# Scan chunks of 64 tokens in a fused Mamba-2 scan and maxout feed-forward kernel

One Trainium2 chip (trn2), one core. The metric is device time in microseconds (us) of that core, lower is better. The kernel before takes 296.08 us (median of 3 runs, 291.53 to 296.67).

## The reference

A state-space scan over 768 tokens (4 batches, 8 heads, head size 32, state size 16), then a feed-forward layer with the maximum of three products. Cut to what matters:

```python
# scan, per chunk of tokens (any chunk length gives the same y)
L = np.exp(cum[:, :, :, None] - cum[:, :, None, :]) * causal
M = np.einsum('bhin,bhjn->bhij', Cc, Bc) * L               # scores and decay
y_intra = np.einsum('bhij,bhjd->bhid', M, xc)              # "own tokens"
y_inter = np.einsum('bhin,bhnd->bhid', Cc, state) * np.exp(cum)[..., None]   # "old state"
state = decay_full * state + sum_j(B_j x_j * decay_from_j) # "new state"
# feed-forward
h = np.maximum(np.maximum(x @ w1, x @ w2), x @ w3)
return h @ w_out
```

## The kernel before

The tokens go through in six blocks of 128 tokens (all four batches, 512 columns), called 0 to 5. For block c+1 the scan is done in between the feed-forward work of block c. The steps of the scan are: transposes of B and C (`trB`, `trC`), scores, decay (loaded as broadcast rows, masked on GpSimd, exponentials on ScalarE), the product of scores and decay on VectorE, old state and own tokens into the y banks (I call the two together the **y visit**), and the new state. Each engine gets its work as one list, in the order of the program, and a piece that has to wait holds up what stands behind it (experiments 3 to 5 show three such cases, in which TensorE waited 0.84 us a block, 3.0 and 1.2 us in the changed kernel). A *bank* is a piece of the memory that TensorE writes its results to, a *tile* of TensorE the part of its array that a `tile_position` names, a *unit* a piece of feed-forward work of some 4.4 us. `Bd` is B times the decay to the end of the chunk (GpSimd), `E` the exponential of the summed decay (ScalarE), `Cd` is C times `E` (VectorE).

The parts that change and that matter here:

```python
    def decay_masks(c, bs):                       # GpSimd
        for b in bs:
            nc.gpsimd.affine_select(out=Ls[c][:, b], in_=Ls[c][:, b], ...)   # 128 x 1024 each

    def decay_part(c, b, g):                      # ScalarE, 4 heads of one batch
        for h in range(g * HALF, (g + 1) * HALF):
            nc.scalar.activation(L[:, b, h], L[:, b, h], AF.Exp, bias=..., scale=1.0)

    def scan_state(c, kind):                      # L456: 16 matmuls, four column tiles
        for b in range(NB):
            for r in range(NP):
                nc.tensor.matmul(out=A[r * PN:(r + 1) * PN, b], lhsT=st["Bd"][:, h:h + 2],
                    rhs=st["x"][:, h:h + 2], tile_position=(0, r * PN), ...)

    def scan_scores(c, b0, banks=None):           # L488: two batches a visit, four row tiles
        for i in range(2):
            for r, s in banks.items():
                nc.tensor.matmul(out=s[:, i], lhsT=st["BT"][rows, b],
                    rhs=st["CT"][rows, b], tile_position=(r * PN, 0), ...)

    def scan_old(c):                              # L511: 16 matmuls of 128 columns
        ...
                nc.tensor.matmul(out=ys[r // 2][q:q + 2 * D, b], lhsT=Sp[rows, b],
                    rhs=st["Cd"][rows, b], start=(b == 0), stop=False,
                    tile_position=(r * PN, q), ...)

    def scan_own(c, bs):                          # L524: 32 matmuls of 128 columns
        for b in bs:
            for h in range(NH):
                t, q = divmod(h, QH)
                nc.tensor.matmul(out=st["y"][t][q * D:(q + 1) * D, b],
                    lhsT=st["x"][:, b * NH + h], rhs=M[:, b, h],
                    tile_position=(0, q * D), ...)
```

(Shapes rearranged and arguments cut where marked by `...`.)

Of the kernel before, what the change touches and what calls it, by code (L numbers as in the profile page):

```python
# [19 lines left out]
def kernel(  # L20
# [19 lines left out]

    nc = tc.nc
# [3 lines left out]
    P = 128  # L45
# [14 lines left out]
    HB = BLK // 2  # L60
    MASKED = -32768.0
# [189 lines left out]


# [9 lines left out]
    def running(rows, lg, out):  # L262
        for w in range(out.shape[1]):
            nc.vector.tensor_tensor_scan(
                out=out[:, w], data0=keep[0:rows], data1=lg[:, w], initial=0.0,
                op0=ALU.mult, op1=ALU.add)

    def from_last(rows, cum, name):

        fj = const.tile(list(cum.shape), FP32, name=name)  # L270
        for w in range(cum.shape[1]):
            nc.scalar.activation(
                fj[0:rows, w], cum[0:rows, w], AF.Exp, bias=cum[0:rows, w, P - 1:P], scale=-1.0)
        return fj
# [20 lines left out]

    Ls = {}

    def decays(c):
        Ls[c] = att.tile([P, NB, NH, P], FP32, tag="L", name="L")
        return Ls[c]  # L300
# [60 lines left out]
    L0, spread = decays(0), {}  # L361
# [6 lines left out]
    running(P, lg0, cum0)  # L368
# [5 lines left out]
    def decay_load(c, pairs=(0, 2)):  # L374
        L = decays(c) if 0 in pairs else Ls[c]
        for b in pairs:
            nc.sync.dma_start(
                out=L[:, b:b + 2].rearrange("j b h i -> j (b h) i"),
                in_=cums[b * NH:(b + 2) * NH, c, :].partition_broadcast(P))
# [7 lines left out]
    def decay_masks(c, bs):  # L387
        for b in bs:
            nc.gpsimd.affine_select(  # L389
                out=Ls[c][:, b], in_=Ls[c][:, b], pattern=[[0, NH], [1, P]],  # L390
                compare_op=ALU.is_ge, fill=MASKED, base=0, channel_multiplier=-1)

    def decay_part(c, b, g):
        L = Ls[c]
        for h in range(g * HALF, (g + 1) * HALF):
            nc.scalar.activation(  # L396
                L[:, b, h], L[:, b, h], AF.Exp,
                bias=ncum[c][:, b * NH + h:b * NH + h + 1], scale=1.0)
# [51 lines left out]
    def scan_state(c, kind):  # L450
        st = blocks[c]
        A = kind([HN, NB, 2, D], "A")
        for b in range(NB):
            for r in range(NP):
                h = b * NH + 2 * r
                nc.tensor.matmul(  # L456
                    out=A[r * PN:(r + 1) * PN, b].rearrange("p g d -> p (g d)"),
                    lhsT=st["Bd"][:, h:h + 2].rearrange("j h n -> j (h n)"),
                    rhs=st["x"][:, h:h + 2].rearrange("j h d -> j (h d)"),
                    start=(b == 0), stop=True, tile_position=(0, r * PN),  # L460
                    skip_group_check=True)
        return lambda: scan_sum(c, A)

    def scan_sum(c, A):
        st = blocks[c]
        states[c + 1] = Sn = att.tile([HN, NB, 2, D], FP32, tag="S", bufs=3, name="S")
        nc.vector.tensor_tensor(  # L467
            out=Sn, in0=A,
            in1=parity.unsqueeze(1).unsqueeze(3).to_broadcast([HN, NB, 2, D]), op=ALU.mult)
        if c > 0:  # L470
            old = att.tile([HN, NB, 2 * D], FP32, tag="old", name="old")
            nc.gpsimd.tensor_tensor(
                out=old, in0=states[c].rearrange("p b g d -> p b (g d)"),
                in1=st["E"][:, :, P - 1:P].to_broadcast([HN, NB, 2 * D]), op=ALU.mult)
            nc.gpsimd.tensor_tensor(  # L475
                out=Sn.rearrange("p b g d -> p b (g d)"),
                in0=Sn.rearrange("p b g d -> p b (g d)"), in1=old, op=ALU.add)

    def scan_scores(c, b0, banks=None):

        st = blocks[c]
        if banks is None:
            banks = {r: att_bank([P, 2, 2, P], "s") for r in range(NP)}
        for i in range(2):
            b = b0 + i
            for r, s in banks.items():
                rows = slice(r * PN, (r + 1) * PN)
                nc.tensor.matmul(  # L488
                    out=s[:, i].rearrange("j g i -> j (g i)"), lhsT=st["BT"][rows, b],
                    rhs=st["CT"][rows, b].rearrange("p g i -> p (g i)"),  # L490
                    start=(i == 0), stop=True, tile_position=(r * PN, 0), skip_group_check=True)
        return banks

    def scan_weight(c, b0, r, s):
        M = Ls[c][:, b0:b0 + 2, 2 * r:2 * r + 2]
        nc.vector.tensor_tensor(out=M, in0=s, in1=M, op=ALU.mult)  # L496

    def scan_weights(c, b0, banks):
        for r, s in banks.items():
            scan_weight(c, b0, r, s)  # L500

    def scan_old(c):

        st = blocks[c]
        st["y"] = ys = [att_bank([P, NB, P], "y") for _ in range(KD)]
        Sp = states[c]
        for b in range(NB):
            for r in range(NP):
                rows = slice(r * PN, (r + 1) * PN)
                q = r % 2 * 2 * D  # L510
                nc.tensor.matmul(  # L511
                    out=ys[r // 2][q:q + 2 * D, b],
                    lhsT=Sp[rows, b].rearrange("p g d -> p (g d)"), rhs=st["Cd"][rows, b],
                    start=(b == 0), stop=False, tile_position=(r * PN, q),
                    skip_group_check=True)

    def scan_own(c, bs):
# [3 lines left out]
        for b in bs:  # L521
            for h in range(NH):
                t, q = divmod(h, QH)
                nc.tensor.matmul(  # L524
                    out=st["y"][t][q * D:(q + 1) * D, b], lhsT=st["x"][:, b * NH + h],
                    rhs=M[:, b, h], start=False, stop=True,
                    tile_position=(0, q * D), skip_group_check=True)
# [17 lines left out]
    def scan_y(c):  # L545
        yT[c] = ffn.tile([P, KD, BLK], FP32, tag="yT", name="yT")
        for t in range(KD):
            nc.scalar.copy(out=yT[c][:, t], in_=blocks[c]["y"][t].rearrange("p b i -> p (b i)"))

    def scan_sums(c):  # L550
# [3 lines left out]
        late = [blocks[c]["y"][k].rearrange("p b i -> p (b i)")[:, r * HB:(r + 1) * HB]  # L554
                for k in range(2) for r in range(2)]
# [4 lines left out]
            for k, (a1, a0) in enumerate((  # L560
                (late[1], y11), (late[3], t[:, 0]), (late[3], y12), (late[2], t[:, 1]))))
# [141 lines left out]
    def hidden_sums(c, eng, fs):  # L703
# [4 lines left out]
        if c not in token_sums:  # L708
            if c < NC - 2:
                t = ffn.tile([P, 3 * NQ, 2, P], FP32, tag="hs", bufs=1, name="hs")  # L710
            else:
                t = att.tile([P, NB, NH, P], FP32, tag="L", name="L").rearrange(
                    "p b (h u) i -> p (b h) u i", u=2)
# [83 lines left out]
    def add_downs(c):  # L797
        if c == 0:
            downs.extend((u, i, f) for u in range(2) for f in range(0, NF, 2) for i in range(2))
        elif c < NC - 2:  # L800
            downs.extend((c, u, which) for u, which in (
                (0, (1,)), (0, (6,)), (0, (5, 7)), (0, (2, 3, 4)), (1, (1, 6)), (1, (5, 7)),
                (1, (2, 3, 4))))
# [85 lines left out]
    running(R, lg, a_sb)  # L889
# [17 lines left out]
    s01 = scan_scores(0, 0)  # L907
    s23 = scan_scores(0, 2, {r: ffn_bank([P, 2, 2, P], "s") for r in (2, 3)})
    state_sum = scan_state(0, att_bank)
    ncums_tp = turned(R, a_sb, "ncums", ffn_bank)  # L910
    scan_weights(0, 0, s01)
# [9 lines left out]
    s23 = scan_scores(0, 2, {r: att_bank([P, 2, 2, P], "s") for r in (0, 1)})  # L921
    sign()
    scan_weights(0, 2, s23)
# [7 lines left out]
    def decay_list(c):  # L931
        return [(c, b + b0, g) for b0 in (0, 2) for g in range(2) for b in range(2)]
# [27 lines left out]
    def transposed(n, both=True):  # L960
# [3 lines left out]
        if n < NC - 1:  # L964
            scan_bd(n)

    def scores(n, b):
        for r, s in scan_scores(n, b).items():
            later.append(lambda r=r, s=s: scan_weight(n, b, r, s))

    for n in range(NF * 3):
# [17 lines left out]
        if n in (13, 14, 16, 17):  # L989
            pop(2)  # L990
# [10 lines left out]
        if n == 1:  # L1001
            fj = from_last(R, a_sb, "fj")
# [10 lines left out]
        if n == 9:  # L1013
            decay_masks(1, (2, 3))
        if n in (5, 7, 9, 11, 13, 14, 15, 16):
# [4 lines left out]
        if n == 12:  # L1020
            scan_e(1)
            scan_cd(1)
            scores(1, 0)
        if n == 15:
            shared["att"] = False
            scores(1, 2)
# [7 lines left out]
    scan_own(1, range(NB))  # L1034
    scan_y(1)
    scan_sums(1)
    later.append(scan_state(1, att_bank))
# [8 lines left out]
    X1 = ["tc", "D", "DD", "s0", "DD", "s2", "A", "y", "DD"]  # L1046
    Y1 = ["", "", "D", "", "", "D", "", "D", ""]
    P1 = [(1, 0, 0), (1, 0, 0), (1, 0, 1), (1, 1, 2), (1, 0, 0), (1, 1, 2), (1, 1, 1), (1, 0, 2),
          (1, 0, 2)]
    D1 = [(0, 0), (0, 0), (2, 0), (2, 0), (2, 0), (2, 0), (0, 2), (0, 1), (0, 2)]  # L1050
    K1 = {0: (0, (0, 1)), 2: (0, (2, 3)), 4: (1, (0, 1)), 6: (1, (2, 3))}
    X2 = ["t", "s0", "D", "s2", "D", "y", "D", "D", "D"]
    Y2 = ["D", "D", "", "", "", "", "", "", ""]
    P2 = [(1, 0, 1), (1, 1, 3), (0, 0, 1), (1, 1, 2), (1, 0, 0), (1, 0, 0), (9, 0, 0), (1, 0, 0),
          (1, 0, 0)]
    D2 = [(0, 0), (1, 0), (1, 0), (1, 0)] + 5 * [(0, 1)]
    K2 = {3: (1, (0, 1)), 5: (1, (2, 3))}
    X3, Y3, P3 = 9 * [""], 9 * [""], 9 * [(1, 0, 0)]

    for c in range(1, NC):  # L1060
# [4 lines left out]
        for k in range(NW):  # L1065
# [20 lines left out]
            elif x == "A":  # L1086
                later.append(scan_state(n, att_bank))
# [5 lines left out]
            elif x == "s0":  # L1093
                scores(n, 0)
            elif x == "s2":
                scores(n, 2)
            elif x == "y":
                scan_old(n)
                scan_own(n, range(NB))
                scan_y(n)  # L1100
                scan_sums(n)
                if 1 < c < NC - 2:
                    later.append(scan_state(n, att_bank))
# [13 lines left out]
            if not (1 < c < NC - 1 and k == 2):  # L1117
                flush()
# [41 lines left out]
```

## Time and profile before

| | before |
|---|---|
| time, median of 3 | 296.08 us (fast 291.53, slow 296.08 and 296.67) |
| span of the profiled (slow) execution | 294.2 us |
| TensorE busy | 283.0 us, 96% |
| TensorE program | 17 packets of instructions on queue 8 |

The program has two kinds of execution. In the slow kind TensorE runs at half clock (granted clock 0.50 in the profile) for 10.24 us near 16 us, which costs about 5 us. The kernel before took 290.5 to 291.8 us without that half clock and 296.1 to 297.1 us with it, so I compare executions with full clock at the start only with each other, and take 291.2 for the kernel before.

### The profile page before, as it was taken

The numbers are of one execution on the slowest core, as the hardware profiler recorded it, in microseconds if no ns is written. First come the engines' busy times: TensorE is split into PE (matmuls) and PEld (weight loads), VectorE is DVE, ScalarE is ACT, GpSimd is POOL, SyncE is SP. The second block draws the span as 40 slices with busy tenths as digits, with TensorE's granted clock in tenths as the row PEclk, the third lists the DMA queues.
The fourth block names the chain that finished last, engine by engine and source line by source line (L and its number), as shares of the span: only waits on it lengthen the run. The fifth ranks groups of instructions, "written<-read, shape, count | busy, mean of one in ns | idle before, by whom it ended". The sixth has DMA issues, their size and how long they took to land.

```text
span 294.2 us, 5768 instructions
## 1 busy us (share of the span) xinstructions
PE 283.0 (96%) x2204; PEld 226.0 (77%) x2204; DVE 214.0 (73%) x427; ACT 119.6 (41%) x323; POOL 113.4 (39%) x132
## 2 busy tenths in 40 slices
PE   6679999999999999999999999999999999999995
PEld 4557435478887788878987878988878988989885
DVE  2752867988698578896867796776897766676682
ACT  3933687834665546333426243335331201011101
POOL 5241638367997535920004940003630203030300
PEclk9957999999999999999999999999999999999999
DMA  7979989989884009971006693001001001000103
GB/s 88 218 255 301 217 144 176 246 171 219 232 140 67 2 21 253 142 88 38 2 0 180 177 128 57 2 0 36 2 0 38 2 1 36 2 1 0 38 0 107
DMA packets 105035, 28.15 MB, mean 96 GB/s; under 512 B 75312, under 2 KB 101936, under 8 KB 105008
## 3 DMA queue, kind: packets, MB, share of 16 engines
q1 hardware_dynamic: 104560, 27.53, 46.5%
q8 instruction: 17, 0.28, 0.4%
q10 hardware_dynamic: 448, 0.26, 0.3%
q14 instruction: 10, 0.08, 0.1%
HBM read 24.54 MB, written 3.24 MB: 94 GB/s over the span
## 4 chain that ended last, share of the span: by engine, by line
PE 84%; DVE 7%; DMA 3%; SPq 2%; issue 1%; ACT 1%; POOL 0%; DVEq 0%; ACTq 0%; POOLq 0%
PE sumB L633 25%; PE sumA L633 18%; PE o L743 16%; PE up L583 8%; PE s L488 4%; PE o L819 4%; PE y L524 3%; DMA raw_x<-in_x_dram 3%; PE y L511 2%; PE up L575 2%; PE y L535 1%; SPq L130 1%; PE A L456 1%; DVE rb L675 1%; DVE m L678 1%
## 5 line engine op out<-in xcount | busy, mean ns | idle before, releaser
L633 PE MATMUL sumA<-yT,w 128*128 128x256 f32 x180 | 55.4, 389 | 0.0
L396 ACT ACTIVATE L<-L,ncums 128x128 f32<-128x128 f32 x160 | 50.2, 393 | 2.5 <-POOL L L389 2.5
L658 ACT COPY eu<-sumA 128x256 f32<-128x256 f32 x45 | 16.8, 373 | 75.3 <-PE sumA L633 68.7
L633 PE MATMUL sumB<-rb 128*128 128x256 f32 x180 | 46.3, 379 | 0.0
L633 PEld LDWEIGHTS sumB<-rb 128*128 128x128 f32 x180 | 34.1, 190 | 4.8 <-DVE rb L558 0.2
L633 PEld LDWEIGHTS sumA<-yT,w 128*128 128x128 f32 x180 | 30.0, 190 | 6.7 <-issue 2.1
L496 DVE TENSOR_TENSOR L<-s,L 128x512 f32<-128x512 f32 x46 | 29.7, 680 | 2.8 <-PE s L488 2.5
L583 PE MATMUL up<-yT,w 128*128 128x512 f32 x64 | 29.1, 600 | 0.2 <-DVE w L193 0.2
L675 DVE TENSOR_TENSOR rb<-sumB,eu 128x512 f32<-128x512 f32 x30 | 20.7, 690 | 11.8 <-PE sumB L633 11.8
L659 DVE TENSOR_TENSOR eu<-sumA,eu 128x256 f32<-128x256 f32 x45 | 18.9, 420 | 14.2 <-ACT eu L658 14.0
L633 PE MATMUL sumB<-yT,rb 128*128 128x256 f32 x90 | 27.9, 391 | 0.3 <-DVE m L661 0.3
L190 POOL TENSOR_TENSOR w_u<-w_u,w_r 128x512 uint32<-128x512 uint32 x12 | 15.3, 1274 | 32.9 <-DVE w_u L184 14.9
L633 PE MATMUL sumA<-rb 128*128 128x256 f32 x90 | 26.8, 379 | 0.0
L633 PE MATMUL sumB<-rb,w 128*128 128x256 f32 x90 | 26.8, 379 | 0.0
L389 POOL TENSOR_SCALAR_AFFINE_SELECT L<-L 128x1024 f32<-128x1024 f32 x20 | 23.6, 1214 | 0.0
L718 POOL TENSOR_TENSOR L<-h 128x256 f32<-128x256 f32 x5 | 3.6, 726 | 50.7 <-DVE h L678 31.7
L583 PEld LDWEIGHTS up<-yT,w 128*128 128x128 f32 x64 | 11.6, 190 | 14.7 <-issue 11.7
L660 DVE TENSOR_TENSOR v<-sumB,eu 128x256 f32<-128x256 f32 x45 | 19.1, 425 | 4.7
L633 PEld LDWEIGHTS sumB<-yT,rb 128*128 128x128 f32 x90 | 15.8, 189 | 6.0 <-DVE m L661 2.3
L475 POOL TENSOR_TENSOR S<-S,old 128x256 f32<-128x256 f32 x4 | 2.9, 730 | 42.9 <-DVE S L467 42.8
L743 PEld LDWEIGHTS o<-wo,h 128*128 128x128 f32 x120 | 15.9, 191 | 4.0 <-DVE ob L752 1.6
L633 PEld LDWEIGHTS sumA<-rb 128*128 128x128 f32 x90 | 17.1, 190 | 2.3
(141 smaller groups left out, 510.0 us busy)
## 6 DMA issues: line engine op xcount, KB each, us to landing
L<-cums SPq DMA_DIRECT2D x10, 1024.0 KB, 9.2
rb<-in_moe_w_dram SPq DMA_DIRECT2D x9, 512.0 KB, 7.5
raw_x<-in_x_dram SPq DMA_DIRECT2D x6, 512.0 KB, 7.6
out_dram<-ob SPq DMA_DIRECT2D x11, 256.0 KB, 2.1
raw_B<-in_B_dram SPq DMA_DIRECT2D x6, 256.0 KB, 4.6
raw_C<-in_C_dram SPq DMA_DIRECT2D x6, 256.0 KB, 6.3
rb<-in_moe_w_out_dram SPq DMA_DIRECT2D x3, 512.0 KB, 6.1
E<-cums SPq DMA_DIRECT2D x40, 32.0 KB, 4.2
```

The source lines that it names most:

```text
L190: nc.gpsimd.tensor_tensor(out=u, in0=u, in1=r, op=ALU.add)
L389: nc.gpsimd.affine_select(out=Ls[c][:, b], in_=Ls[c][:, b], pattern=[[0, NH], [1, P]], compare_op=ALU.is_ge, fill=MASKED, base=0, channel_ ...
L396: nc.scalar.activation(L[:, b, h], L[:, b, h], AF.Exp, bias=ncum[c][:, b * NH + h:b * NH + h + 1], scale=1.0)
L488: nc.tensor.matmul(out=s[:, i].rearrange("j g i -> j (g i)"), lhsT=st["BT"][rows, b], rhs=st["CT"][rows, b].rearrange("p g i -> p (g i)"), ...
L496: nc.vector.tensor_tensor(out=M, in0=s, in1=M, op=ALU.mult)
L583: nc.tensor.matmul(out=bank, lhsT=w_sb[i][:, k, f * P:(f + 1) * P], rhs=yT[0][:, k], start=(k == 0), stop=(k == KD - 1))
L633: nc.tensor.matmul(out=bank[:, half], lhsT=left(p, k), rhs=sides[c][p], start=(first and half == 0), stop=True, skip_group_check=True)
L658: nc.scalar.copy(out=eu[:, 0], in_=A[:, 0])
L659: nc.vector.tensor_tensor(out=eu[:, 1], in0=A[:, 1], in1=eu[:, 0], op=ALU.add)
L660: nc.vector.tensor_tensor(out=v, in0=B[:, 1], in1=eu[:, 1], op=ALU.add)
L675: nc.vector.tensor_tensor(out=t[:, 0:2], in0=B, in1=eu[:, 1:2].to_broadcast([P, 2, HB]), op=ALU.add)
L743: nc.tensor.matmul(out=o[:, PLACES[p]], lhsT=token_sums[c][p][:, f, u], rhs=wo_of(p)[:, f], start=(p == first and f == 0), stop=True, skip ...
```

## The change

**Intent.** Behind block 0, each block of 128 tokens becomes two chunks of 64 tokens. The two chunks lie in the two halves of the 128 partitions, so that matmuls of the upper and of the lower half can use different row or column tiles of TensorE. The square of scores across the halves is not computed any more. In its place a state at the middle of the block (`middle`) is passed from the first chunk to the second. The scores of all four batches are made in one visit. The decay is then half as large, so its loads, masks and exponentials are regrouped.

The diff, cut to its core (comments are mine):

```diff
-    def decay_part(c, b, g):
+    def decay_part(c, r, b0):                       # now 2 heads of 2 batches
...
+    def scan_scores(c):                             # L549 of the changed kernel
+        banks = [att_bank([P, NB, 2, HP], "s") for _ in range(NP)]
+        for b in range(NB):
+            for u in range(2):
+                i = slice(u * HP, (u + 1) * HP)
+                for r, s in enumerate(banks):
+                    nc.tensor.matmul(out=s[i, b], lhsT=st["BT"][rows, b, i],
+                        rhs=st["CT"][rows, b, :, i], tile_position=(r * PN, u * HP), ...)
...
     def scan_state(c, kind):                        # L501: also the middle state
+                for u, A in enumerate(As):
+                    rows = slice(u * HP, (u + 1) * HP)
+                    nc.tensor.matmul(..., lhsT=st["Bd"][rows, h:h + 2],
+                        rhs=st["x"][rows, h:h + 2], tile_position=(u * HP, r * PN), ...)
...
     def scan_old(c):                                # L569: 32 matmuls of 64 columns
+            for u, S in enumerate((states[c], middle[c])):
...
     def scan_own(c):                                # L585: 64 matmuls of 64 columns
         for b in range(NB):
             for h in range(NH):
                 t, q = divmod(h, QH)
-                nc.tensor.matmul(..., rhs=M[:, b, h], tile_position=(0, q * D), ...)
+                for u in range(2):
+                    rows = slice(u * HP, (u + 1) * HP)
+                    nc.tensor.matmul(out=st["y"][t][u][q * D:(q + 1) * D, b],
+                        lhsT=st["x"][rows, b * NH + h], rhs=M[rows, b, h],
+                        tile_position=(u * HP, q * D), ...)
...
     def decay_list(c):
-        return [(c, b + b0, g) for b0 in (0, 2) for g in range(2) for b in range(2)]
+        return [(c, r, b0) for r in range(NP) for b0 in (0, 2)]
...
-        if n == 9:
+        if n == 5:
             decay_masks(1, (2, 3))                  # block 1: second masks earlier
```

The order of work in the units between is changed to suit: the state comes two or three units ahead of the y visit, and the masks of later blocks come earlier.

## The prediction

> **What bounds the kernel now.** I read the page first (busy shares, clock row), then the groups of instructions with shapes kept apart, the chain of waits in order of time, the waits of TensorE, and last the timeline of TensorE around one block of the scan.
>
> ```profile
> PE 283.0 (96%) x2204; PEld 226.0 (77%) x2204; DVE 214.0 (73%) x427; ACT 119.6 (41%) x323; POOL 113.4 (39%) x132
> ...
> PEclk9957999999999999999999999999999999999999
> ...
> 15.80:26.00 10.20, 9.49 (x107) 6.32 (x96) 4.21 (x8) 2.38 (x5) 3.18 (x3) 0.50 0.82 262
> ...
> 115.90:160.90 45.00, 44.63 (x380) 37.81 (x379) 34.62 (x71) 18.01 (x55) 14.32 (x12) 1.00 0.42 77
> ```
>
> TensorE is busy 96% of the span and 44.6 of every 45.0 us in the steady blocks (the window row of 115.9 to 160.9), so nearly only TensorE time counts. The clock is half from 15.8 to 26 us (0.50): ten microseconds in which TensorE does half the work, some 5 us lost, in this execution. That explains the three times of before, two near 296 and one 291.5.
>
> The change touches four groups of matmuls, all of the scan, behind the first block:
>
> ```profile
> L488 PE MATMUL s<-CT,BT 32*128 32x256 f32 x192 | 15.5, 410 | 1.4 <-ACT CT L430 1.4
> ...
> L524 PE MATMUL y<-L,raw_x 128*32 128x128 f32 x320 | 9.8, 274 | 0.0
> ...
> L511 PE MATMUL y<-Cd,S 32*64 32x128 f32 x160 | 5.5, 274 | 0.0
> ...
> L456 PE MATMUL A<-raw_x,Bd 128*32 128x64 f32 x160 | 3.5, 230 | 1.9 <-DMA raw_x<-in_x_dram 1.9
> ```
>
> The mean of one (410 ns) is its latency, not its cost. 320 records of L524 for 5 blocks of 32 calls show that an fp32 matmul is two instructions. Their cost is read from the timeline, from one start to the next:
>
> ```profile
> 135.34 1.10 PE L511 MATMUL y<-Cd,S 32*64 32x128 f32 x32
> 136.37 1.95 PE L524 MATMUL y<-L,raw_x 128*32 128x128 f32 x64
> 138.14 0.63 PE L456 MATMUL A<-raw_x,Bd 128*32 128x64 f32 x32
> 138.70 0.70 PE L633 MATMUL sumA<-yT,w 128*128 128x256 f32 x2
> ...
> 115.85 1.15 PE L488 MATMUL s<-CT,BT 32*128 32x256 f32 x16
> 116.93 0.70 PE L633 MATMUL sumA<-yT,w 128*128 128x256 f32 x2
> ```
>
> So: old state (L511) 1.03 us, own tokens (L524) 1.77, new state (L456) 0.56, scores (L488) 1.08 each of two visits. The yardstick is a row of the chain of waits:
>
> ```profile
> 114.19 0.87 PE sumA L633 x4
> ...
> 120.89 1.34 PE o L743 x12
> ```
>
> Four instructions of 256 columns over the whole array take 0.87 us, twelve of 128 columns 1.34: 0.85 ns a column (0.87 where each has its own weights of as many columns), so about 215, 108 and 54 ns for 256, 128 and 64 columns. Own tokens are 64 instructions of 128 columns; one after the other they would take 6.9 us, and they take 1.77: four column tiles run side by side. The scores, 16 of 256 columns, would take 3.4 and take 0.86 plus a margin: four row tiles side by side.
>
> [...] This trace agrees for four tiles (6.9 us against 1.77); it has no run with eight tiles, on which the change rests. [...] This trace has L456: 32 starts in 0.41 us, 13 ns each[...]. [...] the last full matmul before the scores stays 0.31 us ahead instead of 0.215, and the visit ends 0.22 us over its 0.86: 0.2 to 0.3 us a visit. [...] here the half clock starts at 15.8 us, behind the 1.9 us wait for raw_x and the 1.4 us wait for CT. The change touches nothing before that, so I expect both kinds of execution again.
>
> **Scores.** Before, two visits a block: 2 x (1.08 + 0.10 ahead) = 2.36 us. After, one visit of 32 calls, 64 instructions of 128 columns, at eight positions (four row tiles x two halves of the columns): half the arithmetic, because the square across the halves is gone. 64 / 8 x 108 = 0.86, with margins 1.2 us. Saved 1.15 us a block, 5.7 us over five blocks.
>
> **Own tokens.** After: 64 calls, 128 instructions of 64 columns over two row halves x four column tiles: 128 / 8 x 54 = 0.86 us with 0.2 margin, against 1.89 where no state follows. Saved 0.8 us a block, 4.0 us in all. The halves write different banks (four y banks instead of two).
>
> **Old state.** 64 instructions of 64 columns, but still four positions (the half changes only the columns): 64 / 4 x 54 = 0.86, as before. Nothing.
>
> **New state.** 64 instructions of 64 columns at eight positions: 8 x 54 = 0.43, as before. But the visit now stands alone, with its margins 0.7 us, and the last block needs one too (for the middle): 5 x 0.7 = 3.5. Before: three behind the own tokens, 0.44 more than these without (1.77 + 0.56 - 1.89), and one alone with 0.68: 2.0 us. Added 1.5 us.
>
> **Sum on TensorE**: -5.7 - 4.0 + 1.5 = -8.2 us.
>
> **Beside it.** VectorE: 40 products of scores and decay (0.68 us each) become 20, -13.6 us, and five more head selections (0.41 each) come, +2. GpSimd: five more steps of the state, 0.62 + 0.73 each, and one more Bd (1.1), +7.9 us at 39% busy; the masks stay 20 of 1024 elements, about 1.2 us each. ScalarE: 160 exponentials of 64 columns in place of 128, less; the copies of y become 20 of 256 (0.37) from 10 of 512 (0.59). The decay loads fall from 10 of 1024 KB to half the bytes. None of this is on the path, except where VectorE holds TensorE up: the chain leaves TensorE between 123.5 and 130 us for VectorE, and "DVE ob L752", "DVE m L661" and "DVE rb L661" are behind 1.6, 2.3 and 1.3 us of idle weight loads. With 2.3 us less of VectorE work a block I count 1.5 us in all. Against it I set 1 us for new waits: the state through the middle goes VectorE, GpSimd, VectorE, GpSimd (about 0.41 + 1.35 + 1.35 us plus queueing), which has some three units of 4.4 us before its reader; and the first sums now read the copied y instead of its bank.
>
> -8.2 - 1.5 + 1.0 = -8.7 us, from 296.1 to about 287.
>
> **Rivals.** (a) **Eight tiles do not run side by side**: if only four do, own tokens take 128 / 4 x 54 = 1.73 as before, scores 64 / 4 x 108 = 1.73 + 0.3 against 2.36, and the state doubles its 0.43. Then -1.7 + 1.5 + 2.2, and the time stays near 296 to 298. For it: no record of eight, and pairs of weight load and matmul start some 6.8 ns apart in the trace, so eight need 54 ns, exactly what 64 columns last. [...] (b) **Instruction supply**: the scan's y visit grows from 192 to 384 TensorE instructions, in 2.1 us instead of 2.8. The page's instruction queue shows 17 packets of 16 KB, one for about 256 instructions, each 0.9 to 1.5 us. If it can't keep up it costs up to 1 us a visit: -8.7 becomes about -4, 292. (c) **A new wait**: the y matmuls wait for the middle state, or the state for its two banks. GpSimd is in order, and masks that wait for late decay rows could hold the state back; 1 us a block would give 292 as well. For it: GpSimd gets the most new work and its sums of hidden values block it 7.3 us at the start of each block. Against it: decay rows are half the bytes, and the schedule gives the state three units.
>
> **Range and chances.** The main way gives 287, in the fast kind of execution some 4.5 us less, about 282.5; (b) or (c) in the slow kind gives 292. I weigh the main way 0.7, (b) and (c) together 0.2, (a) 0.1. So 287 us, 281.5 to 292.5; faster by over 2% 0.72 (8.7 of 296 is 2.9%), within 2% 0.25, slower by over 2% 0.03.
>
> **What would show it.** In the profile after: one scores visit of 64 instructions in about 1.2 us a block; 128 own-token instructions in about 1.05; 64 of the old state in about 1.03; the state in about 0.7; a steady block of some 43 us in place of 45.0; VectorE some 11 us less. If own tokens take 1.7 us, (a) is right. If the matmuls of the y visit keep gaps without a semaphore, (b). If the waits name S, middle or a GpSimd line ahead of y, (c). The prediction is wrong if these visits don't shrink, or if they do and the time is lost again in waits on VectorE or GpSimd.

## More of the kernel before

The prediction shows the lines of the profile; two more rows of the page matter later (queue: packets, MB, share of the DMA engines; and the loads of the decay rows: count, KB each, us to landing):

```profile
q8 instruction: 17, 0.28, 0.4%
...
L<-cums SPq DMA_DIRECT2D x10, 1024.0 KB, 9.2
```

## The result

The changed kernel takes 304.71 us (median of 4 runs, 303.99 to 305.28; mean clocks 0.987 to 0.989, and full clock at the start in the profiled one). The ratio of the fast runs is 1.0463, 95% interval 1.0423 to 1.0503: slower. A ratio is the mean time of one kernel's fast runs over that of the other's of the same rounds, so it is not quite the ratio of the medians quoted.

The page of the changed kernel: busy shares, the clock in 40 slices of 7.6 us, the instruction queue and the decay loads.

```profile
PE 280.5 (92%) x3004; PEld 225.7 (74%) x3004; DVE 206.2 (68%) x414; ACT 112.5 (37%) x335; POOL 121.4 (40%) x143
...
PEclk9999999968999999999999999999999999999999
...
q8 instruction: 23, 0.38, 0.5%
...
L<-cums SPq DMA_DIRECT2D x20, 256.0 KB, 6.1
```

TensorE is busy for less time than before (280.5 against 283.0 us) but the span is longer. Half clock is in both figures: half of the 9.49 us that TensorE was busy at half clock before, and half of 5.89 us after. Without it some 278.3 and 277.5 us of work are left, an estimate from these windows. So the loss is waiting and half clock, not more work. The clock is low in slices 9 and 10, at about 61 to 76 us, and nowhere at the start. There are 23 packets of instructions instead of 17.

The four groups, and their visits in the timeline of TensorE (start, length, count of instructions):

```profile
L585 PE MATMUL y<-L,raw_x 64*32 64x64 f32 x640 | 7.8, 229 | 4.3 <-issue 4.3
L549 PE MATMUL s<-CT,BT 32*64 32x128 f32 x320 | 6.4, 279 | 0.9 <-DVE Cd L459 0.9
L569 PE MATMUL y<-Cd,S 32*64 32x64 f32 x320 | 5.8, 220 | 0.0
L501 PE MATMUL A<-raw_x,Bd 64*32 64x64 f32 x288 | 4.2, 223 | 2.2 <-POOL Bd L464 2.2
```

```profile
122.87 1.21 PE L549 MATMUL s<-CT,BT 32*64 32x128 f32 x64
124.01 0.48 PE L695 MATMUL sumA<-yT,w 128*128 128x256 f32 x1
...
143.29 1.16 PE L569 MATMUL y<-Cd,S 32*64 32x64 f32 x64
144.38 1.48 PE L585 MATMUL y<-L,raw_x 64*32 64x64 f32 x128
145.79 0.70 PE L695 MATMUL sumA<-yT,w 128*128 128x256 f32 x2
```

From start to start the scores take 1.14 us in one visit, the old state 1.09, the own tokens 1.41. A new state without its wait takes 0.79 (blocks 1 and 2 of this run). So scores and own tokens shrank, the old state stayed, the new state grew about as foreseen, and the time went elsewhere. I cut the span at the starts of the y visits (block number in brackets):

| stretch | before | after | difference |
|---|---|---|---|
| start to y(1) | 60.46, about 55.5 without the slow start | 57.03 | about +1.5 |
| y(1) to the transposes of block 2 | 3.36 | 7.58 | +4.2 |
| from there to y(2) | 35.63 | 43.14 | +7.5 |
| y(2) to y(5) | 125.55 | 125.70 | +0.15 |
| y(5) to the end | 69.23 | 70.02 | +0.8 |

Nearly everything is lost around block 1. The chain of waits in order of time (start, length, what) shows the first loss:

```profile
57.10 1.09 PE y L569 x64
58.19 1.15 PE y L585 x75
59.34 4.35 issue
63.70 0.51 PE y L585 x13
```

In the middle of the own tokens TensorE stands for 4.35 us and waits for no semaphore ("issue"). No other block has that. Half clock follows (columns: stretch, its length, busy time of five engines, granted clock, DMA share, GB/s):

```profile
63.02:69.85 6.83, 5.89 (x40) 4.75 (x40) 1.79 (x5) 2.46 (x7) 1.58 (x3) 0.50 0.65 91
```

TensorE was busy for 5.89 of these 6.83 us (the first 0.7 us are still the gap), so about 3 us are lost by half clock (in it, two matmul instructions of 256 columns took 0.85 us from start to start, at 67.23 us; behind it, at 71.56 us, 0.43). The list of waits (engine, line, releaser: total us, times, longest) has what is new of the rest:

```profile
PE y L585 <- issue: 4.3, 1, 4.3
...
PE sumA L695 <- ACT m L734: 2.9, 1, 2.9
...
PE A L501 <- POOL Bd L464: 2.2, 3, 0.8
...
PE up L645 <- DVE w L197: 1.4, 2, 1.1
...
PE s L549 <- DVE Cd L459: 0.9, 1, 0.9
```

The second of these falls in block 1, and the chain of waits shows where it comes from:

```profile
101.46 1.16 POOL L L404
...
102.68 1.75 POOL L L404
...
104.45 1.06 ACT L L414 x4
105.52 0.26 ACT m L734
...
105.82 1.13 PE sumA L695 x4
```

GpSimd makes two masks (L404), ScalarE has the exponentials of just those rows next in its order (L414), the copy of a bank (`m`, L734) stands behind them, and TensorE needs that bank free. Of the third stretch's 7.5 us, this wait is 3.0, the half clock some 2.6 (its 5.2 us behind 64.6 us) and the wait of the scores for Cd 1.2, both waits taken from start to start; the last 0.7 us I did not take apart.

In the steady blocks the gain is there and is spent. Start to start on TensorE, y(3) to y(4), 45.15 us before and 45.22 after:

| | before | after | prediction |
|---|---|---|---|
| scores | 2.15 | 1.14 | 2.36 to 1.2, with lead-ins |
| own tokens | 1.77 | 1.41 | 1.89 to 1.05 |
| old state | 1.03 | 1.09 | same |
| new state | 0.56 | 0.87 | +0.3 |
| all other groups with their waits | 39.63 | 40.71 | less |

The four visits give 1.00 us a block, and the other groups take 1.07 back, of which the wait for `Bd` is 0.84.

### The profile page after: what moved, and what is told of

It reads as the page before. It is cut to its first block, busy times and chain, and to the rows that moved or that the text cites. A ratio compares the mean times of both kernels' runs of the same rounds, so it can differ in the third digit from the quotient of the medians.

```text
span 303.5 us, 7400 instructions
## 1 busy us (share of the span) xinstructions
PE 280.5 (92%) x3004; PEld 225.7 (74%) x3004; DVE 206.2 (68%) x414; ACT 112.5 (37%) x335; POOL 121.4 (40%) x143
## 4 chain that ended last, share of the span: by engine, by line
PE 64%; DVE 13%; POOL 12%; issue 4%; DMA 2%; ACT 2%; SPq 1%; POOLq 0%; DVEq 0%; ACTq 0%
PE sumB L695 18%; PE o L805 13%; PE sumA L695 12%; PE up L645 6%; POOL L L404 3%; DMA E<-cums 2%; PE y L585 2%; PE y L569 2%; POOL hs L786 2%; DVE rb L737 2%; PE o L881 1%; POOL hs L780 1%; PE A L501 1%; PE spread L336 1%; PE up L637 1%
## 5 line engine op out<-in xcount | busy, mean ns | idle before, releaser
L780 POOL TENSOR_TENSOR hs<-h 128x256 f32<-128x256 f32 (+1 forms) x8 | 9.2, 1148 | 105.1 <-DVE h L740 105.1
L414 ACT ACTIVATE L<-L,ncums 128x64 f32<-128x64 f32 x160 | 41.6, 338 | 11.7 <-POOL L L404 11.7
L695 PEld LDWEIGHTS sumA<-yT,w 128*128 128x128 f32 x180 | 30.7, 192 | 9.2 <-ACT m L734 3.3
L404 POOL TENSOR_SCALAR_AFFINE_SELECT L<-L 128x1024 f32<-128x1024 f32 (+1 forms) x20 | 25.2, 1259 | 0.7
L695 PEld LDWEIGHTS sumB<-rb,w 128*128 128x128 f32 x90 | 17.1, 190 | 2.3
L805 PE MATMUL o<-wo,h 128*128 128x128 f32 x120 | 17.6, 280 | 0.6 <-DVE ob L814 0.6
```

What stands on the lines that cost most here:

```text
L404: nc.gpsimd.affine_select(out=Ls[c][0:rows, b], in_=Ls[c][0:rows, b], pattern=[[0, len(bs)], [0, NH], [1, HP]], compare_op=ALU.is_ge, fill ...
L414: nc.scalar.activation(L[:, b, h], L[:, b, h], AF.Exp, bias=ncum[c][:, b * NH + h:b * NH + h + 1], scale=1.0)
L695: nc.tensor.matmul(out=bank[:, half], lhsT=left(p, k), rhs=sides[c][p], start=(first and half == 0), stop=True, skip_group_check=True)
L780: eng.tensor_tensor(out=s1, in0=a21, in1=a22, op=ALU.add)
L805: nc.tensor.matmul(out=o[:, PLACES[p]], lhsT=token_sums[c][p][:, f, u], rhs=wo_of(p)[:, f], start=(p == first and f == 0), stop=True, skip ...
```

## The experiments

**Theory.** (1) The gap is instruction supply. The trace of the changed kernel has 23 packets of 16 KB on the instruction queue for 6050 TensorE instructions, one for 263 on average (17 for 4451 before, one for 262), and the 4.35 us gap ended 1.2 us after one of them had landed (61.01 to 62.46 us). What follows is my reading, for the experiments to test: a packet holds 256 instructions, the gap stands at a border between two packets, and the next packet is asked for when the border before it is passed, 256 instructions earlier (so counted, the 23 packets start from 1.9 us before to 6.1 us after TensorE passes that border), so if 256 instructions go by faster than a packet takes to come, TensorE stands. (2) The other losses are orders: a piece of new work stands on GpSimd or ScalarE ahead of one that TensorE needs (the waits of 0.84, 3.0 and 1.2 us above). **Rivals.** The gap comes from eight tiles or the halved banks themselves, or from the mere length of the visit; eight tiles do not run side by side; or the waits only cover others, and taking one away shows the next.

Where the borders lie I read off from the one gap of the changed kernel. In y(1) they are 77 and 333 instructions behind its start, of 384. The other y visits have one border inside. Experiments 1, 2 and 7 move the borders and so test that reading. Runs 1 to 7 are single executions; each tells whether its start had half clock.

### 1. The borders moved by 104 instructions

```diff
+        if b0 == 0:
+            for _ in range(52):    # 104 instructions, 1 column each, overwritten later
+                nc.tensor.matmul(out=banks[0][0:D, 0, 0, 0:1], lhsT=ident16[:, 0:D],
+                    rhs=mask[:, 0:1], start=True, stop=True, ...)
```

> The changed kernel with 104 tiny TensorE instructions (52 weight loads and matmuls of one column) ahead of the first scores, at some 12 us, nothing else changed: the scan of block 1 lies 104 instructions later in the program. Theory (instruction supply): TensorE gets its program in pieces of 256 instructions; in the changed kernel a piece border lies 77 and the next 333 instructions into the y visit of block 1, so the second piece is asked for only some 2 us before it is needed and comes 4.4 us too late. Shifted by 104 the borders lie at -26 and 230: the gap of 4.35 us in the own tokens goes, the half clock behind it (6.8 us at half speed, 3.4 us lost) goes too, and the time falls by some 7 us, 304.7 to about 297.5. Rival (a wait that the profile doesn't show, or eight tiles that jam): the gap stays where it is and the time stays at 305 to 306.

Measured: 306.81 us, full clock at the start. The gap of block 1 is gone and so is the half clock behind it. But the same shift puts two borders into all later y visits. In y(3), y(4) and y(5) (108/364, 52/308 and 61/317) new gaps stand (the fence shows y(1) and y(3)):

```profile
57.97 1.48 PE L590 MATMUL y<-L,raw_x 64*32 64x64 f32 x128
...
139.75 1.40 PE L590 MATMUL y<-L,raw_x 64*32 64x64 f32 x119
142.88 0.32 PE L590 MATMUL y<-L,raw_x 64*32 64x64 f32 x9 [1.74 <-issue]
```

They cost 1.9, 2.25 and 1.8 us, and no half clock followed them (granted clock 1.00 from 142.8 to 150.0 us, behind the first of them; mean clock of the run 0.994). In y(2) (40/296) there is none: its packet started at 101.41 us, 1.8 us before TensorE came to the border ahead. A half clock of 3.4 us, near 100 us, is new as well. The position was right and the time was a miss: I had not checked where the borders fall in the later blocks. That the gap moves with the borders, while code, tiles and banks of the visit stay, speaks against the rivals.

### 2. The borders moved by 200

```diff
-            for _ in range(52):
+            for _ in range(100):
```

> The same with 200 tiny instructions: the borders lie at 134 and 390 of the 384 instructions of the y visit of block 1. Theory (instruction supply): the piece from 390 on is asked for inside the visit and needed right after its end, so a gap of some 4 us comes back, now behind the last own token and ahead of the transposes or of the first products, with a half clock behind it; time 304 to 307. Rival (extra work early on is what removed the gap of e1): the gap is gone here too and the time is 1 to 2 us above e1.

Measured: 314.20 us, with half clock at the start and at two more places (mean clock 0.956), so the time is not compared. The gap stands where the borders say, six instructions behind the visit, in the transposes (fence: timeline of TensorE):

```profile
65.28 1.48 PE L590 MATMUL y<-L,raw_x 64*32 64x64 f32 x128
67.07 0.55 PE L433 MATMUL trB<-ident,raw_B 128*128 128x128 f32 x3 [0.31 <-ACT yT L617]
71.08 0.37 PE L433 MATMUL trB<-ident,raw_B 128*128 128x128 f32 x1 [3.46 <-issue]
```

So it does not belong to the own tokens at all. It belongs to the 256 instructions before it having gone by quickly, in 2.05 us.

### 3. Bd ahead of the sums of hidden values on GpSimd

```diff
             if k == 0 and c > 1:
+                if n < NC:
+                    scan_bd(n)
                 hidden_sums(...)
```

(and the call behind the transposes taken away). In the changed kernel `Bd` stands behind 7.3 us of other GpSimd work.

> The changed kernel with the product Bd of the next block put ahead of the four sums of hidden values in GpSimd's order (blocks 2 to 4 of the loop). Theory (in-order GpSimd): the state visits of the blocks 3 to 5 wait 0.8 to 0.95 us each for Bd, which stands behind 7.3 us of sums; with Bd ahead these waits go and with them some 0.1 us of restart each: -2.5 to -3 us, 302. The sums come 1.1 us later, which their readers (five units later) don't notice. Rival (the wait only moves to the sums): the output products wait in its place and the time stays within 0.5 us of 304.7.

Measured: 301.25 us, full clock at the start, so 3.4 us less. The wait of L501 for `Bd` is gone from the list. The three steady blocks give 2.4 us of the 3.4 (34.90, 44.30 and 44.11 us in place of 35.54, 45.22 and 44.94). The rest is luck: in this run the gap of block 1 was 2.8 us in place of 4.4, its half clock 3.4 us long in place of 6.8, and a half clock of 3.4 us came in addition behind the wait for ScalarE.

### 4. The decay made in the order of the masks

```diff
     def decay_list(c):
+        if c > 2:
+            return [(c, r, b0) for b0 in (0, 2) for r in range(NP)]
         return [(c, r, b0) for r in range(NP) for b0 in (0, 2)]
```

> The changed kernel with the old order of the decay exponentials for the blocks 3 to 5 (first batches 0 and 1 of all heads, then 2 and 3). Theory (in-order ScalarE behind GpSimd): at 102 us TensorE waits 3.0 us for a copy of ScalarE that stands behind an exponential of block 3, which waits for the second mask of GpSimd; in the old order the first exponentials need the first mask only, so this wait goes: -3 us, about 301.5. Rival: GpSimd is simply late here and the next reader of the masks or sums waits in its place; the time stays within 0.7 us of 304.7.

Measured: 304.28 us, but with 10.2 us of half clock at the start, and with a gap of 1.9 us in place of 4.4. Half clock followed this gap too (granted clock 0.50 from 67.4 to 70.6 us). The wait of the sums for ScalarE, 2.9 us before, is no longer in the list. What it is worth in time could not be read from this run, which is why experiment 9 repeats it.

### 5. The exponential of E one unit earlier

```diff
-            if n < NC and k == 2 * int(c == 1):
+            if n < NC and k == int(c == 1):
                 scan_e(n)
```

> The changed kernel with the exponential of E for block 2 asked for one unit earlier (behind the first unit of block 1 instead of the second or third), nothing else. Theory (in-order ScalarE behind the masks): in the changed kernel the scores of block 2 wait 1.1 to 1.3 us for Cd, because ScalarE reaches the exponential of E late; here that wait falls under 0.4 us and the time by about 1.2 us, to 303.5. Rival: the scores only wait for something else that lands at the same moment, and the time stays at 304.7.

Measured: 306.10 us, again with half clock at the start (some 301 without), and with a gap of 2.3 us. The wait of the scores for Cd is gone from the list; a wait of 0.38 us for VectorE stands in the next unit. The time proves nothing by itself.

### 6. Own tokens on four tiles in a row

```diff
-                for u in range(2):            # innermost: upper, lower, upper, ...
+            for u in range(2):                # outside the heads: 8 upper, then 8 lower
```

> The changed kernel with the order of the own tokens changed: all heads of the upper rows of a batch, then all heads of the lower rows, so that only four tiles follow each other (before: eight). Instructions, borders and everything else are the same. Theory: eight tiles do run side by side[...], so with four tiles of 54 ns the visit becomes bound by the tiles, 13.5 ns a pair: 128 x 13.5 = 1.75 us in place of 1.42, five visits, +1.6 us, 306.3 (less where block 1 waits for instructions anyhow). Rival (tiles side by side were never eight, only four): the visit keeps 1.42 us and the time stays at 304.7.

Measured: 306.94 us, with a gap of 4.9 us in block 1. The undisturbed visits (here block 4):

```profile
191.05 1.57 PE L585 MATMUL y<-L,raw_x 64*32 64x64 f32 x128
192.56 0.70 PE L695 MATMUL sumA<-yT,w 128*128 128x256 f32 x2
```

1.51 us in place of 1.41. Both are below the 128 / 4 x 54 = 1.73 us that four tiles alone would need, so more than four tiles run side by side in both kernels, and the rival of the prediction is wrong. Experiment 7 has the same count on four tiles, 128 instructions of 64 columns, and measures 2.00 us where a full matmul follows as here (blocks 2 and 5), and 1.81 where the new state does. My 1.75 was wrong too. That the lower rows start while the upper ones still run, so that even this order uses eight tiles in part, would fit the 1.51, but no run shows it apart.

### 7. The kernel before, with its matmuls cut into halves of the columns

```diff
-                nc.tensor.matmul(out=st["y"][t][q * D:(q + 1) * D, b], ..., rhs=M[:, b, h])
+                for i in (slice(0, P // 2), slice(P // 2, P)):
+                    nc.tensor.matmul(out=st["y"][t][q * D:(q + 1) * D, b, i], ...,
+                        rhs=M[:, b, h, i])
```

(the same for the old state). This has the instruction count of the changed y visit with the arithmetic, the four tiles and the banks of the kernel before.

> The kernel BEFORE, with each matmul of the old state and of the own tokens split into two of 64 columns: same arithmetic, same four tiles, same banks, same decay and order, but twice the instructions in the y visit, which puts two borders of 256 instructions into the y visit of block 1 (14 and 270 instructions behind its start). Theory (instruction supply): a gap of 1 to 4.5 us without any semaphore appears inside the own tokens of block 1, which the kernel before does not have, and the kernel loses at least that much: 293 to 296 in the fast state where the kernel before has 291.5. Rival (the gap comes from eight tiles, the halves of the rows or the banks of the change, not from the number of instructions): no gap in that visit, and within 1 us of the kernel before.

Measured: 294.76 us with clock 0.999, where the kernel before takes 290.64 and 291.56: 3.7 us slower. The gap did not come where I expected it. Block 1 passed: its packet started early, at 55.84 us, and landed at 57.25, 1.2 us before TensorE came to its border (58.44), which the table below shows to be just in time. y(5) has two borders too (36/292) and no gap, its packet having started 1.0 us before the border ahead. A gap came in block 3, behind the y visit, in the state:

```profile
134.90 0.31 PE L456 MATMUL A<-raw_x,Bd 128*32 128x64 f32 x7
136.39 0.54 PE L456 MATMUL A<-raw_x,Bd 128*32 128x64 f32 x23 [1.18 <-issue]
```

The gap is 1.3 of the 3.7 us; the y visits, 0.2 us longer each (3.03 against 2.80 in block 3), are another 1.2, and the rest I did not trace. So a higher instruction count alone makes such a gap (one gap in one run), without eight tiles and without the new banks. And "two borders in one visit" is only a rule of thumb; what counts in these runs is the time of 256 instructions (1.5 to 2.05 us at the gaps) against the time of the packet. The DMA records of the instruction queue give that for the gaps (times in us; the packet lasts 0.9 to 1.5; the gaps are good to some 0.2 us, idle time being a little less and the distance of the starts a little more):

| run, place | packet starts | lands | TensorE goes on | after landing | gap |
|---|---|---|---|---|---|
| changed kernel, y(1) | 61.01 | 62.46 | 63.70 | 1.24 | 4.4 |
| 6, y(1) | 61.22 | 62.71 | 63.94 | 1.23 | 4.9 |
| 4, y(1) | 64.01 | 64.97 | 66.36 | 1.39 | 1.9 |
| 1, y(3) | 140.45 | 141.50 | 142.88 | 1.38 | 1.9 |
| 1, y(4) | 187.73 | 188.66 | 190.16 | 1.50 | 2.25 |
| 1, y(5) | 234.66 | 235.60 | 237.07 | 1.47 | 1.8 |
| 2, transposes | 67.79 | 69.28 | 71.08 | 1.80 | 3.6 |
| 7, new state of block 3 | 133.73 | 135.13 | 136.39 | 1.25 | 1.3 |

In each case TensorE goes on 1.2 to 1.8 us after the packet has landed, 2.35 us or more after it started; the packet started 0.6 to 3.9 us after TensorE had passed the border ahead. The traces hold a stricter test of the reading. In all eight cases the first instruction behind the gap has a number of the form 256 n + 193 among TensorE's instructions. Counted so, all 13 traces have just as many borders as packets, and in none of 284 cases did TensorE pass a border less than 1.2 us after its packet had landed.

The gap of the changed kernel is the longest but for its twin in experiment 6, because its packet started more than 3 us after TensorE had passed the border before it. Five runs (the changed kernel and experiments 3 to 6) have this border at the same instruction. Where the DMA engines were busy for 1.0 of the microsecond behind it (the changed kernel, 6), the packet started 3.4 and 3.9 us after it; where they were busy for 0.48, 0.19 and 0.56 (3, 4, 5), after 1.9, 1.1 and 1.3 us, and the gap was 2.8, 1.9 and 2.3 us. That busy DMA engines delay the packet fits this, but no run changed the loads alone.

### 8. No y visit with two borders

Experiment 1 with 110 instructions, and 130 more of the kind ahead of the scores of block 2, so that the borders are at -32/224, -96/160, -28/228, -84/172 and -75/181.

```diff
+        if c == 2:
+            for _ in range(65): ...
```

> The changed kernel with 110 tiny instructions ahead of the first scores of block 0 and 130 ahead of the scores of block 2 (TensorE waits there anyhow), chosen so that no y visit has two borders of 256 instructions inside it: borders at -32/224/480, -96/160/416, -28/228/484, -84/172/428, -75/181/437 of 384. Theory (instruction supply): no gap without a semaphore over 0.8 us in any y visit, no half clock at 63 us; against the changed kernel this gives back 4.4 us of gap and about 3 us of half clock, less 1 us for the added instructions: about 298. Rival 1 (the gap is due to the length of the visit, not to where the borders fall): a gap stays in block 1 or in another y visit. Rival 2 (the time is held elsewhere, for example by VectorE and the loads, so the gap hides another wait): the gaps go, but the time stays over 302.

Measured: 300.57 and 301.18 us with full clock at the start, 305.70 and 306.26 with half clock there. No gap stands in any y visit, and no half clock at 63 us. Against the fast runs of the changed kernel it gives 3.8 us back, less than the 6.7 expected. Two terms account for most of the missing 2.9. The 130 instructions take 1.7 us (78.13 to 79.84 us in the timeline of experiment 10), not the 1 us allowed for all; in part they fill the wait for Cd, which is gone from the list. And a half clock of 3.4 us, worth 1.7, comes behind the wait for ScalarE, which is still in the list of waits:

```profile
PE sumA L705 <- ACT m L744: 2.9, 1, 2.9
```

### 9. The same with the decay in the order of the masks

> The kernel without gaps (tiny instructions at both places) and with one mend alone: the decay of blocks 3 to 5 is made in the order in which the masks come. The run of this mend by itself fell in an execution with half clock at the start and with a different gap, so it is repeated on this base. Theory (GpSimd masks, then ScalarE's exponentials, then TensorE's sums): the wait of the sums for ScalarE of 3.04 us in block 1 falls under 0.5 us and with it the half clock of 3.4 us behind it goes, so 300.9 - 3.0 - 1.7 = 296.2 in the fast state. Rival: the wait only moves to another place in the same block, and the time stays over 299.

Measured: 296.07 us at full clock throughout, 299.89 at a mean clock of 0.987, 301.38 with the slow start. The profiled run (slow start) has no wait of the sums for ScalarE and no half clock later. The full-clock run is 4.8 us faster than the kernel of experiment 8, as expected; it is one run, and the 299.89 beside it, which counts as fast too but lost clock somewhere, was not profiled.

### 10. All mends together

Experiments 3, 4, 5 and 8 in one kernel.

> All mends together: the 110 and 130 tiny instructions that keep two borders out of every y visit, Bd ahead of the hidden sums on GpSimd, the decay of the later blocks in the order in which the masks come, and the exponential of E one unit earlier. If the causes add up, in the fast state: 300.9 (the kernel with the tiny instructions alone) - 3.4 (Bd, as measured) - 3.0 (wait of the sums for ScalarE) - 1.7 (the half clock of 3.4 us behind that wait) - 1.2 (wait of the scores) = 291.6, within 1 us of the fast kernel before (291.1), and no half clock behind the start. If the waits are only links of one chain, so that taking one away shows the next (VectorE, loads), it ends at 295 or more.

Measured: 294.00 and 293.77 us with full clock throughout (before: 291.17 to 291.83), 298.66 and 299.14 with the slow start. The sum of parts had promised 291.6, so 2.3 us are missing. 1.0 of them is the luck in experiment 3 that I had counted as the worth of `Bd`. And the step for E was counted on top of tiny instructions that already stood in that wait, so it could give nothing more. What remains of the change's own cost is 1.4 us of waits of the up-projection for VectorE ahead of block 1, and the 1.7 us of tiny instructions.

### 11. Two more mends

The 65 matmuls ahead of the scores of block 2 go to four tiles in turn, and the second masks of block 1 go back to their old place (with the exponentials of block 1 in the order of its masks, not shown):

```diff
-        if n == 5:
+        if n == 9:
             decay_masks(1, (2, 3))
```

> The kernel with all mends, with two more: the 65 tiny matmuls ahead of the scores of block 2 go to four tiles in turn (so 130 instructions cost about 0.6 us in place of 1.8), and the second masks of block 1 go back to where the kernel before has them (its decay is made by batches again), so that one of two pairs of masks no longer runs beside the decoding of the weights. Theory: -1.2 for the tiny instructions, -1.0 for the wait of the up matmuls for VectorE of 1.27 us: 293.9 - 2.2 = 291.7 in the fast state, level with the kernel before (291.5). Rival: the decoding is held by VectorE itself, and the wait stays; then 292.7. If a gap without a semaphore opens behind the scores of block 2 (309 instructions behind the first tiny one), it is about 1 us more.

Measured: 292.11, 292.21, 292.47 and 292.81 us, all with full clock, where the kernel before takes 290.54 to 291.20. The ratio of the fast runs is 1.0056 (1.0029 to 1.0083); under the bar of 2% the verdict is "unclear", but the interval leaves no room for a gain. The wait for VectorE (L197) fell, and a wait of the scores of block 1 (at 45 us) for ScalarE took most of its place:

```profile
PE s L560 <- ACT CT L448: 1.2, 1, 1.2
...
PE up L656 <- DVE w L197: 0.2, 1, 0.2
```

A gap of 0.4 us is left in y(1); its packet started 4.65 us after the border ahead. This is the best version of the change that I found, and it is still 0.6% behind the kernel before.

Put in a row, fast runs: 304.7 (changed), 300.9 (borders), 296.1 (and order of the decay, one run), 293.9 (and Bd, E), 292.4 (and cheaper instructions, masks). The kernel before: 290.5 to 291.8.

## Why the prediction was wrong

The prediction was 287.0 us, faster. The kernel is at 304.7. The step that failed is the sum "-8.2 - 1.5 + 1.0". It left the supply of instructions out, as a rival with a small chance, and that cost 7.4 us (gap 4.4, half clock behind it 3.0). It allowed 1.0 us for new waits, and they cost 8.0. The visits gave 5 of the 8.2 us, and VectorE's 1.5 did not come. Step by step:

- **Scores, -1.15 us a block: right.** One visit of 1.14 us where two of 1.08 and their lead-ins stood.
- **Own tokens, -0.8 us a block: direction right, size wrong.** "128 / 8 x 54 = 0.86 us with 0.2 margin" measured 1.41. Rival (a) is refuted by the 1.81 to 2.00 us that the same count took on four tiles (experiment 7; 1.73 by the estimate). The first 32 matmuls start 7.7 ns apart, near the 6.8 that eight tiles of 54 ns allow. The later ones start 10.7 ns apart on average, many in turns of 6 and 11 and some at 17. There is no semaphore in between. That pairs of weight load and matmul are handed out no faster is my guess; no run settled it.
- **Old state, 0: right** (1.03 to 1.09). **New state, +1.5 in all: right** (+0.3 a block, 0.2 without its wait).
- So the four visits give 1.0 to 1.1 us a block instead of 1.65.
- **VectorE's relief, -1.5: did not come.** VectorE is busy 8 us less (11 foreseen), but its waits are not where its work shrank. The idle time that I read, 1.6, 2.3 and 1.3 us, was that of weight loads, which run beside matmuls (226.0 us of loads and 283.0 of matmuls in a span of 294.2); the matmuls themselves waited for those lines only 1.0 us (`ob`) and 0.3 us (`m`) in the whole kernel before. In the kernel with all mends the other groups of block 3 to 4 take 39.87 us against 39.63 before. I divided a saving of busy time over waits without asking which wait it stands ahead of.
- **Rival (b), "up to 1 us a visit", chance 0.2 together with (c): the right mechanism, mis-sized, and the step that failed most.** I had the packet count and the packet's duration, 0.9 to 1.5 us, and spread the cost over visits. What counted was the single place where 256 instructions went by (in 1.5 us at this gap) in less time than their next packet took. From the packet's start to TensorE going on it took 2.35 us or more, and where loads kept the DMA engines busy the packet started over 3 us late as well. The gap was 4.4 us, and the half clock behind it another 3.0; I had thought of half clock at the start only.
- **Rival (c), new waits, +1.0: right in kind, too small.** I looked for the wait at the middle state, and it never appeared. The waits came from the regrouping that I had called "None of this is on the path": masks ahead of exponentials ahead of a copy (3.0, and in other runs a half clock of 1.7), `Bd` behind the sums (0.8 in each of three blocks), E (1.2), and masks beside the decoding of the weights (1.4). I had named "GpSimd is in order, and masks that wait for late decay rows could hold the state back" and then followed only the state, not the ScalarE queue behind the masks.

The sum with the measured terms: visits -5, gap +4.4, half clock +3.0, ScalarE wait +3.0, Bd +2.4, E +1.2, decoding waits +1.4, which makes +10.4. The measured difference is 13.5 (304.7 against 291.2). Some 3 us are spread over waits under 0.5 us each, among them 0.8 us behind y(5), and I did not take them apart.

## What to carry to other kernels

Before you cut matmuls into smaller ones to fill more tiles, count instructions per microsecond: where TensorE ran through 256 of them in about 2 us (1.5 to 2.05 us at ten gaps of these runs), it came to the next border before the packet, unless the packet had started early (four passages of 1.7 to 2.2 us without a gap). Where the border falls changes with an edit far ahead (104 instructions at 12 us took the gap out of y(1) and put three into later visits, experiment 1). Work taken off VectorE (8 us less busy), which is not the bound here, was worth nothing; what moved in the order of GpSimd and ScalarE cost more (8.0 us of waits) than TensorE's visits saved (5 us). Follow each moved piece of GpSimd and ScalarE work to whatever stands behind it in the same queue, up to TensorE.
